# Products with v, and the transposes of their results, on two 64-row tiles with a bank each

## The chip, the core and the metric

One core of a Trainium2 chip runs the whole program in one launch. The metric is the device time of an execution in microseconds. The kernel before was timed in three runs: 2619.9, 2620.06 and 2625.03 us, median 2620.06 us. The profile is of one more execution.

## The reference

Eight sequences of 2496 rows (u and v with 256 columns, z with 64) go through an attention without softmax, and the rows that come out through a mixture of eight experts with a fixed capacity.

```python
scores = (1 / S) * np.matmul(z, z.transpose(0, 2, 1))
attn = np.maximum(scores, 0.0) ** 2
x = (u * np.matmul(attn, v)).reshape(B * S, D)
...
logits = x @ w_gate            # tokens go to experts in order of logit, at most N / E to each
out[mask] = np.maximum(x[mask] @ w1[e], 0.0) @ w2[e]
```

## The kernel before, in words

**Attention** (the first 1480 us). The work is cut into 40 groups: for each sequence b, five blocks g of queries (four of 512, one of 448). A group runs over 20 key tiles; one key tile of one group is a *step*, and there are 800 steps. I number the steps of a group 0 to 19. Every float32 product is made of two or three products of fp32r parts, a high part and what it leaves.

- `scores` (L772) makes the scores of four steps at once, four steps ahead of their use. z has 64 columns, so a key tile fills 64 rows of the array; two key tiles stand on the two halves of the rows and write to two PSUM banks. A batch is six such pairs of matmuls. Its four banks are the pool "sc".
- ScalarE turns them into `r` (relu, L790) and `a` (square, L795). `split_hi` (L798) rounds `a` to `hi`, on ScalarE for three steps of five and on VectorE for two; `split_lo` (L806) makes `lo = a - hi` on VectorE. There are three buffers of `a` and four each of `hi` and `lo`.
- `av` (L815) adds a step's products with v to two accumulators `acc0` and `acc1`, one for each half of v's 256 columns: vh·hi (L825), vh·lo (L827), vl·hi (L828), all 128 rows deep. Step 19 has no `lo` of its own and makes four matmuls, the others six. Each accumulator has two buffers, so that the next group writes to another bank.
- When a group is over, `take_acc` (L830) copies acc0 on ScalarE and acc1 on VectorE to `at0` and `at1`. Two steps later `turn_back` (L839) transposes them in eight 128x128 pieces to two sc banks, `post_mul` (L851) multiplies by u into `xs`, a DMA stores it, and `post_logits` (L868) makes 32 products `lt` of 256 columns with w_gate's rows on VectorE (L876), which are spread over the group's later steps.
- Once in a sequence `z_turn` (L730) transposes the next z in five parts, and `split_v` (L758) makes the 20 pairs `vh` (ScalarE) and `vl` (VectorE) of the next v.

The order of work is set twice: by the step for which `at(n, ...)` files each piece, and then by the framework's scheduler, which at build time gives every engine a queue of its own from that order and its own estimates. Each engine then works its queue off in order and waits where an operand or a buffer is missing.

**Experts** (from about 1480 us). For each expert VectorE searches the logits for a threshold and makes the list of its tokens: tiles `oa`, `ob` and `hl` (L415 to L425) hold one-hot codes of the rank of 40 columns of tokens each. `QW` (L201) is the number of columns that lie side by side in them: the 128 weights of one column, and the 40 numbers that move past them, are QW elements apart. 156 matmuls (L431) an expert add them up to the list. For the first expert this is on the path; for the others it runs beside the expert before, whose rows are gathered, multiplied by w1 and w2 and scattered.

Of the kernel before, what the change touches and what calls it, by code (L numbers as in the profile page):

```python
# [8 lines left out]
F32 = mybir.dt.float32  # L9
# [4 lines left out]
AF = mybir.ActivationFunctionType  # L14
# [81 lines left out]
def moe(tc, xd, first, jp, identf, w1, w2, out, B, S, cp):  # L96
    nc = tc.nc
    E, D, F = w1.shape
    NT = S // 128
    TL = S - NT * 128  # L100
    KT = NT + 1
    NG = KT // 4
    DH = D // 128
# [16 lines left out]
    with ExitStack() as ctx:  # L120
# [3 lines left out]
        ps = ctx.enter_context(tc.tile_pool(name="ps2", bufs=2, space=PSUM))  # L124
# [73 lines left out]
        nc.vector.tensor_copy(idl, idh_i)  # L198

        CB = JP // 4  # L200
        QW = 4  # L201
        QN = CB // QW
        slot = rp.tile([128, 128, QW], BF, name="slot")
        nc.gpsimd.iota(slot, pattern=[[1, 128], [0, QW]], base=0, channel_multiplier=0,  # L204
# [382 lines left out]
        todo = {}  # L587
# [4 lines left out]
        for k in range(E):  # L592
            for g in range(NG):
                n0 = (k * NG + g) * FT
# [7 lines left out]
            n0 = k * PER  # L602
# [46 lines left out]
def attention(tc, u, v, z, w_gate, xd, identf, made, first, scale):  # L649
    nc = tc.nc  # L650
    B, S, D = u.shape
    DQ = z.shape[-1]
    lg, m = first["lg"], first["m"]
    E = lg.shape[2]
    NT = S // 128
    TL = S - NT * 128
    KT = NT + 1
    DH = D // 128
# [5 lines left out]
    SCB = 4  # L664
    with ExitStack() as ctx:
# [3 lines left out]
        wk = ctx.enter_context(tc.tile_pool(name="wk", bufs=3))  # L669
        ps = ctx.enter_context(tc.tile_pool(name="ps", bufs=2, space=PSUM))  # L670
# [3 lines left out]
        def load_gate():  # L674
            wgb = wk.tile([128, E, D], F32, name="wgb", bufs=1)
            for h in range(2):
                wg = wk.tile([128, DH, 128 * E // 2], F32, name="wg", tag="xs")
                wg = wg.rearrange("p a b -> p (a b)")
                nc.sync.dma_start(wg, bass.AP(tensor=w_gate.tensor, offset=w_gate.offset + h * 128 * E,
                                              ap=[[0, 128], [1, 128 * E]]))  # L680
                with in_turn(0):
                    nc.vector.tensor_copy(wgb[:, :, h * 128:(h + 1) * 128], wg.rearrange("p (d e) -> p e d", e=E))
            wgt = wk.tile([128, DH, E], F32, name="wgt", bufs=1)
            nc.sync.dma_start(wgt, w_gate.rearrange("(h p) e -> p h e", h=DH))
            WG.update(rows=wgb, cols=wgt)
# [5 lines left out]
        ZH, ZL, ZI, ZP, VR, VH, VL, UR = {}, {}, {}, {}, {}, {}, {}, {}  # L691
        XS, ACC, AT, SC, R, A, HI, LO = {}, {}, {}, {}, {}, {}, {}, {}
# [76 lines left out]
        def width(g):  # L769
            return min(512, S - 512 * g)  # L770
# [35 lines left out]
        def split_lo(n):  # L806
            a, h = A.pop(n), HI[n]
            if seq[n][2] == NT:
                nc.vector.tensor_sub(h[TL:], a[TL:], h[TL:].bitcast(F32))
                return  # L810
            l = wk.tile([128, 512], F32R, name="lo", bufs=4)[:, :width(seq[n][1])]
            recent["l"] = nc.vector.tensor_sub(l, a, h.bitcast(F32))  # L812
            LO[n] = l

        def av(n):  # L815
            b, g, kt = seq[n]
            if kt == 0:
                ACC[b, g] = [ps.tile([128, 512], F32, name=f"acc{d}") for d in range(2)]
            last = kt == NT
            h, l = HI.pop(n), LO.pop(n, None)  # L820
            for d in range(2):
                o = ACC[b, g][d][:, :width(g)]
                c = slice(d * 128, (d + 1) * 128)
                vh, vl = VH[b, kt][:, c], VL[b, kt][:, c]
                nc.tensor.matmul(o, vh, h, start=(kt == 0), stop=False)  # L825
                if not last:
                    nc.tensor.matmul(o, vh, l, start=False, stop=False)  # L827
                nc.tensor.matmul(o, vl, h, start=False, stop=last)  # L828

        def take_acc(b, g, d):  # L830
            t = wk.tile([128, 512], F32, name=f"at{d}", bufs=2)[:, :width(g)]
            o = ACC[b, g][d][:, :width(g)]
            if d:
                nc.vector.tensor_copy(t, o)
            else:
                nc.scalar.activation(t, o, AF.Copy)
            AT[b, g, d] = t

        def turn_back(b, g):  # L839
            for half in range(2):  # L840
                p = ps.tile([128, 512], F32, name="sc", bufs=SCB)
                for i in range(2 * half, 2 * half + 2):
                    c = slice(i * 128, (i + 1) * 128)
                    if 4 * g + i == NT:
                        c = slice(i * 128 + TL - 128 * (b % 2) - TL * (1 - b % 2), i * 128 + TL)
                    for d in range(2):
                        o = p[:c.stop - c.start, (i % 2) * D + d * 128:(i % 2) * D + (d + 1) * 128]
                        nc.tensor.transpose(o, AT[b, g, d][:, c], identf)
                ACC[b, g][half] = p

        def post_mul(b, g, half):  # L851
            if half == 0:
                XS[b, g] = wk.tile([128, 4, D], F32, name="xs")
            acc = ACC[b, g][half].rearrange("p (i d) -> p i d", d=D)
            full = NT - 4 * g - 2 * half
            cuts = [(0, 2, 128)] if full >= 2 or b % 2 else [(0, full, 128), (full, 2, TL)]
            for i, j, n in cuts:
                c = slice(2 * half + i, 2 * half + j)
                nc.vector.tensor_mul(XS[b, g][:n, c], acc[:n, i:j], UR[b, g][:n, c])
            if half == 1:  # L860
                xs = XS[b, g]
                n = min(4, NT - 4 * g)
                nc.sync.dma_start(xd[b * S:b * S + NT * 128].rearrange("(p i) d -> p i d", i=NT)[:, 4 * g:4 * g + n],
                                  xs[:, :n])
                if n < 4:
                    nc.sync.dma_start(xd[b * S + NT * 128:(b + 1) * S], xs[TL * (b % 2):TL * (b % 2) + TL, n])
# [38 lines left out]
            best_expert(nc, wk, first, slice(lo, hi), eq[:, :hi - lo])  # L905
            order_keys(nc, first, slice(lo, hi))

        todo = {}

        def at(n, f, *a):  # L910
            todo.setdefault(n, []).append((f, a))
# [4 lines left out]
        for b in range(B):  # L916
            for g in range(NQ):
                n0 = (b * NQ + g) * KT
                m0 = n0 + KT
                t = m0 + (0 if m0 == B * NQ * KT else 2)  # L920
                for d in range(2):
                    at(m0, take_acc, b, g, d)
                at(t, turn_back, b, g)
                for d in range(2):
                    at(t + 1, post_mul, b, g, d)
                for e in range(4 * E if m0 < B * NQ * KT else 0):
                    at(t + 2 + e * (KT - 7) // (4 * E), post_logits, b, g, e // E, e % E)
                if b or g:
                    at(n0 - 3, load_u, b, g)
            n0 = b * NQ * KT  # L930
            if b == B - 1:
                at(B * NQ * KT + 2, last_logits, b, NQ - 1)
                at(B * NQ * KT + 3, settle, b * NT + 4 * (NQ - 1), (b + 1) * NT)
                at(B * NQ * KT + 3, settle, B * NT, J)
            if b:
                for g in range(NQ):
                    m = n0 - 3 * KT + 4 * g
                    at(m - 4, load_z, b, g)
                    at(m, z_turn, b, g)
                    at(n0 - KT + 4 * g - 8, load_v, b, g)  # L940
                at(n0 - 3 * KT + 4 * NQ + 2, swap_z, b, slice(0, KT * 128))
                for kt in range(KT):
                    at(n0 - KT + kt, split_v, b, kt)
            else:
                for kt in range(KT):
                    at(kt - 4, split_v, 0, kt)
                for g in range(1, NQ):
                    at(4 * g - LA - 1, z_turn, 0, g)
                    at(4 * g - LA, swap_z, 0, slice(512 * g, 512 * g + 512))
                    if g >= 3:  # L950
                        at(4 * g - 13, load_z, 0, g)
                        at(4 * g - 11, load_v, 0, g)
# [13 lines left out]
        start = min(min(todo), -LA)  # L966
        for n in range(-LA, N + 4 * E):
            if n == 2:
                early.close()
            if n % 4 == 0 and 0 <= n + LA < N:  # L970
                scores(n + LA)
            if 0 <= n + LA < N:
                rectify(n + LA)
            if 0 <= n + 2 < N:
                square(n + 2)
            if 0 <= n + 1 < N:
                split_lo(n + 1)
            if 0 <= n + 2 < N:
                split_hi(n + 2)
            for k in sorted(k for k in todo if k < n):  # L980
                for f, a in todo.pop(k):
                    f(*a)
            if 0 <= n < N:
                av(n)
            for f, a in todo.pop(n, []):
                f(*a)
# [25 lines left out]
```

## Time and profile before

| | us |
|---|---|
| median of three runs | 2620.06 |
| the profiled execution | 2624.11 |
| its span in the profile | 2622.1 |
| PE busy | 2540.4 |
| DVE busy | 1992.1 |
| ACT busy | 1523.7 |

The profiled execution is 4 us above the median, and inside the three runs. A matmul's time in the profile is from its start to its modelled end; matmuls overlap, so that what one costs is the distance from its start to the next one's. In the same way VectorE and ScalarE start an instruction before the one ahead has quite ended, and the cost of one is again the distance between starts. "x2" in a row of the timeline is two instructions that start together or follow each other.

### The profile page before, as it was taken

How to read it: one execution, taken by the hardware profiler on the slowest of the kernel's cores; microseconds unless marked ns; L12 is line 12 of the kernel's file. 1: busy time of each engine (PE TensorE's matmuls, PEld its weight loads, DVE VectorE, ACT ScalarE, POOL GpSimd, SP SyncE). 2: the span in 40 equal slices, each digit the busy share in tenths (PEclk: the TensorE clock that was granted, in tenths of full speed). 3: DMA queues.
4: the chain of work that ended last, by engine and by line, in shares of the span. 5: the costliest groups of instructions: out<-in, count | busy, mean ns of one | idle time of the engine just before them, and what ended most of it. 6: DMA issues, size and time to landing. Idle time of an engine off the chain costs nothing.

```text
span 2622.1 us, 44527 instructions
## 1 busy us (share of the span) xinstructions
PE 2540.4 (97%) x16035; PEld 2091.9 (80%) x16035; DVE 1992.1 (76%) x6127; ACT 1523.7 (58%) x2941; POOL 361.0 (14%) x506
## 2 busy tenths in 40 slices
PE   8999999999999999999999749999999999999998
PEld 6777777777777777777777638888989898999997
DVE  6888788887898888887888768958595969696322
ACT  7788787787787887878877412323233333233332
POOL 2000000000000000000000003233333333333331
PEclk9999999999999999999999859999999999999999
DMA  4121220220121211212100011212121212121110
GB/s 139 41 79 48 57 62 32 63 72 31 49 72 39 66 58 37 72 48 57 39 25 25 16 41 49 69 41 67 41 71 39 74 39 73 39 90 55 45 43 24
DMA packets 71645, 139.60 MB, mean 53 GB/s; under 512 B 12160, under 2 KB 39680, under 8 KB 71424
## 3 DMA queue, kind: packets, MB, share of 16 engines
q1 hardware_dynamic: 56320, 95.84, 12.2%
q0 software_dynamic: 15104, 40.91, 5.0%
q8 instruction: 126, 2.06, 0.3%
q14 instruction: 95, 0.78, 0.1%
HBM read 85.60 MB, written 40.89 MB: 48 GB/s over the span
## 4 chain that ended last, share of the span: by engine, by line
PE 82%; DVE 12%; ACT 3%; issue 2%; DMA 1%; POOL 0%; POOLq 0%; ACTq 0%; SPq 0%; DVEq 0%
PE acc L825 13%; PE acc L828 11%; PE acc L827 11%; PE sc L782 11%; PE hp L514 5%; PE y L545 5%; PE y L547 5%; PE y L546 5%; PE hp L515 5%; PE hp L516 5%; DVE lt L876 3%; DVE lo L812 2%; PE srch L431 2%; PE srch L230 2%; PE xp L499 1%
## 5 line engine op out<-in xcount | busy, mean ns | idle before, releaser
L812 DVE TENSOR_TENSOR lo<-a,hi 128x512 fp32r<-128x512 f32 (+1 forms) x760 | 508.4, 673 | 191.9 <-ACT hi L801 186.5
L825 PE MATMUL acc<-hi,vh 128*128 128x512 f32 (+1 forms) x1600 | 645.9, 404 | 1.8 <-ACT hi L801 1.8
L828 PE MATMUL acc<-hi,vl 128*128 128x512 f32 (+1 forms) x1600 | 617.9, 386 | 0.0
L827 PE MATMUL acc<-lo,vh 128*128 128x512 f32 (+1 forms) x1520 | 589.2, 388 | 0.5 <-DVE lo L812 0.2
L795 ACT ACTIVATE a<-r 128x512 f32<-128x512 f32 (+1 forms) x800 | 492.0, 631 | 145.4 <-DVE lo L812 145.4
L533 ACT ACTIVATE hh<-hp 128x512 fp32r<-128x512 f32 (+1 forms) x320 | 188.0, 588 | 562.2 <-PE hp L516 478.3
L876 DVE SCALAR_TENSOR_TENSOR lt<-xs,wgb 128x256 bf16<-128x256 f32 x1248 | 464.0, 415 | 0.5
L790 ACT ACTIVATE r<-sc 128x512 f32<-128x512 f32 (+1 forms) x800 | 426.9, 589 | 62.9 <-PE sc L782 60.5
L825 PEld LDWEIGHTS acc<-hi,vh 128*128 128x128 f32 x1600 | 300.7, 188 | 121.5 <-issue 39.5
L545 PE MATMUL y<-w2h,hh 128*128 128x256 f32 (+1 forms) x1280 | 365.1, 285 | 0.0
L546 PE MATMUL y<-w2l,hh 128*128 128x256 f32 (+1 forms) x1280 | 361.6, 283 | 0.0
L828 PEld LDWEIGHTS acc<-hi,vl 128*128 128x128 f32 x1600 | 300.9, 188 | 57.3 <-issue 0.9
L827 PEld LDWEIGHTS acc<-lo,vh 128*128 128x128 f32 x1520 | 286.3, 188 | 51.0 <-DVE lo L812 5.0
L801 ACT ACTIVATE hi<-a 128x512 fp32r<-128x512 f32 (+1 forms) x480 | 292.7, 622 | 57.8 <-PE acc L828 55.8
L514 PE MATMUL hp<-xh,w1h 128*128 128x512 f32 (+2 forms) x646 | 262.0, 406 | 0.3 <-ACT xh L507 0.3
L515 PE MATMUL hp<-xl,w1h 128*128 128x512 f32 (+2 forms) x646 | 250.4, 388 | 0.0
L516 PE MATMUL hp<-xh,w1l 128*128 128x512 f32 (+2 forms) x646 | 249.2, 386 | 0.0
L545 PEld LDWEIGHTS y<-w2h,hh 128*128 128x128 f32 (+1 forms) x1280 | 240.0, 188 | 10.3
L546 PEld LDWEIGHTS y<-w2l,hh 128*128 128x128 f32 (+1 forms) x1280 | 240.0, 187 | 9.1
L578 POOL DMA_INDIRECT out_dram<-y,idx x160 | 181.5, 1134 | 389.0 <-ACT y L572 341.5
L446 POOL DMA_INDIRECT xg<-xd,idx x160 | 160.9, 1006 | 397.9 <-PE xp L499 140.6
L204 POOL IOTA slot<- 128x512 bf16 x1 | 1.2, 1211 | 1455.1 <-DVE nrem L278 1455.1
(1144 smaller groups left out, 3793.1 us busy)
## 6 DMA issues: line engine op xcount, KB each, us to landing
vr<-in_v_dram SPq DMA_DIRECT2D x32, 512.0 KB, 3.7
ur<-in_u_dram SPq DMA_DIRECT2D x32, 512.0 KB, 4.4
xd<-xs SPq DMA_DIRECT2D x32, 512.0 KB, 2.9
wr<-in_moe_w_dram SPq DMA_DIRECT2D x32, 512.0 KB, 5.2
zh<-zh SPq DMA_DIRECT2D x14, 320.0 KB, 4.0
zl<-zl SPq DMA_DIRECT2D x14, 320.0 KB, 6.1
zin<-in_z_dram SPq DMA_DIRECT2D x31, 128.0 KB, 2.0
vr<-in_v_dram SPq DMA_DIRECT2D x8, 384.0 KB, 3.3
```

What stands on the lines that cost most here:

```text
L514: nc.tensor.matmul(p[:, c], wh, xh, start=(d == 0), stop=False)
L515: nc.tensor.matmul(p[:, c], wh, xl, start=False, stop=False)
L516: nc.tensor.matmul(p[:, c], wl, xh, start=False, stop=(d == DH - 1))
L545: nc.tensor.matmul(o, h[:, c], wh, start=first, stop=False, skip_group_check=True)
L546: nc.tensor.matmul(o, h[:, c], wl, start=False, stop=False, skip_group_check=True)
L790: recent["r"] = nc.scalar.activation(r, p, AF.Relu, scale=scale)
L795: nc.scalar.activation(a, R.pop(n), AF.Square)
L812: recent["l"] = nc.vector.tensor_sub(l, a, h.bitcast(F32))
L825: nc.tensor.matmul(o, vh, h, start=(kt == 0), stop=False)
L827: nc.tensor.matmul(o, vh, l, start=False, stop=False)
L828: nc.tensor.matmul(o, vl, h, start=False, stop=last)
L876: nc.vector.scalar_tensor_tensor(t[r], XS[b, g][r, i], 1.0, WG["rows"][r, e], op0=OP.mult, op1=OP.mult, accum_out=lg[r, j, e:e + 1])
```

## The change

The accumulators become four, each with one buffer: for either half of v's columns one bank for rows 0 to 63 of the key tile and one for rows 64 to 127. Every product with v is two matmuls on the two halves of the rows. `take_acc` becomes `take_even`, which copies the two banks of the lower half on ScalarE and is called ahead of the scores of the group's next batch, and `add_odd`, which adds the banks of the upper half to the copies on VectorE. `turn_back` transposes pieces of 64 rows, 16 a group, each half of the rows to a bank of its own, and `post_mul` reads a bank with a step. The pieces of `split_v` and the loads of v are filed over a longer stretch. `at0`, `at1`, `xs` and `wg` have fewer buffers. `QW` goes from 4 to 2.

```diff
-        QW = 4
+        QW = 2
...
-                ACC[b, g] = [ps.tile([128, 512], F32, name=f"acc{d}") for d in range(2)]
+                ACC[b, g] = [[ps.tile([128, 512], F32, name=f"acc{d}{s}", bufs=1) for s in range(2)] for d in range(2)]
...
-                vh, vl = VH[b, kt][:, c], VL[b, kt][:, c]
-                nc.tensor.matmul(o, vh, h, start=(kt == 0), stop=False)
-                if not last:
-                    nc.tensor.matmul(o, vh, l, start=False, stop=False)
-                nc.tensor.matmul(o, vl, h, start=False, stop=last)
...
+                for v, x in ((VH, h), (VH, l), (VL, h)):
+                    for s in range(2) if x is not None else ():
+                        r = slice(64 * s, 64 * s + 64)
+                        nc.tensor.matmul(ACC[b, g][d][s][:, :w], v[b, kt][r, c], x[r], start=(kt == 0 and v is VH and x is h),
+                                         stop=(last and v is VL))
+
+        def take_even(b, g):
+            for d in range(2):
+                t = wk.tile([128, 512], F32, name=f"at{d}", bufs=1)[:, :width(g)]
+                nc.scalar.activation(t, ACC[b, g][d][0][:, :width(g)], AF.Copy)
+                AT[b, g, d] = t
+
+        def add_odd(b, g):
+            for d in range(2):
+                t = AT[b, g, d]
+                nc.vector.tensor_add(t, t, ACC[b, g][d][1][:, :width(g)])
...
+                for d in range(2):
+                    for s in range(2):
+                        r = slice(64 * s, 64 * s + 64)
+                        nc.tensor.transpose(views[s][:c.stop - c.start, i, d], AT[b, g, d][r, c], identf[r, r])
...
-                XS[b, g] = wk.tile([128, 4, D], F32, name="xs")
+                XS[b, g] = wk.tile([128, 4, D], F32, name="xs", bufs=2)
...
-                    at(n0 - KT + 4 * g - 8, load_v, b, g)
+                    at(n0 - KT - 6 + 7 * g, load_v, b, g)
...
-                    at(n0 - KT + kt, split_v, b, kt)
+                    at(n0 - KT + 2 + 17 * kt // 10, split_v, b, kt)
...
+            if n in ends:
+                take_even(*ends[n])
             if n % 4 == 0 and 0 <= n + LA < N:
                 scores(n + LA)
...
+            if n in ends:
+                add_odd(*ends[n])
             if 0 <= n + 2 < N:
                 split_hi(n + 2)
```

The queues of the engines move with it. On VectorE, in the group b = 3, g = 1 of the kernel before, from the `lo` of step 6 to the `lo` of step 10 (`lt` are the products with w_gate of the group before; right ahead of these rows stand the two `xs` and three `lt`):

```order
L812 TENSOR_TENSOR lo<-a,hi 128x512
L876 SCALAR_TENSOR_TENSOR lt,lg<-xs,wgb 128x256 x2
L812 TENSOR_TENSOR lo<-a,hi 128x512
L876 SCALAR_TENSOR_TENSOR lt,lg<-xs,wgb 128x256 x6
L803 CAST hi<-a 128x512
L876 SCALAR_TENSOR_TENSOR lt,lg<-xs,wgb 128x256
L812 TENSOR_TENSOR lo<-a,hi 128x512
L803 CAST hi<-a 128x512
L876 SCALAR_TENSOR_TENSOR lt,lg<-xs,wgb 128x256
L812 TENSOR_TENSOR lo<-a,hi 128x512
L876 SCALAR_TENSOR_TENSOR lt,lg<-xs,wgb 128x256 x2
L812 TENSOR_TENSOR lo<-a,hi 128x512
```

With the change, on the same engine in the same group, from the first `lt` behind the two `xs` (the `lo` of step 6 now stands ahead of `xs`) to the `lo` of step 10:

```order
L878 SCALAR_TENSOR_TENSOR lt,lg<-xs,wgb 128x256 x6
L812 TENSOR_TENSOR lo<-a,hi 128x512
L878 SCALAR_TENSOR_TENSOR lt,lg<-xs,wgb 128x256 x13
L803 CAST hi<-a 128x512
L878 SCALAR_TENSOR_TENSOR lt,lg<-xs,wgb 128x256
L812 TENSOR_TENSOR lo<-a,hi 128x512
L878 SCALAR_TENSOR_TENSOR lt,lg<-xs,wgb 128x256 x4
L803 CAST hi<-a 128x512
L878 SCALAR_TENSOR_TENSOR lt,lg<-xs,wgb 128x256
L812 TENSOR_TENSOR lo<-a,hi 128x512
L878 SCALAR_TENSOR_TENSOR lt,lg<-xs,wgb 128x256 x6
L812 TENSOR_TENSOR lo<-a,hi 128x512
```

Of the 32 `lt` of a group, 15 stood ahead of the `lo` of step 10 and 31 stand there now. In the other groups that follow a finished one it is 31 in 24 of 39, 30 in seven, 28 in one, and 25 with six `vl` in the seven groups in which v is split.

On ScalarE, at the end of that group in the kernel before, the batch of the next group's steps 0 to 3, up to the copy of acc0 (the two `r` behind it are of the batch after):

```order
L790 ACTIVATE r<-sc 128x512 x2
L795 ACTIVATE a<-r 128x512
L790 ACTIVATE r<-sc 128x512 x2
L795 ACTIVATE a<-r 128x512
L801 ACTIVATE hi<-a 128x512
L795 ACTIVATE a<-r 128x512 x2
L801 ACTIVATE hi<-a 128x512 x2
L836 ACTIVATE at_8279<-acc_7812 128x512
L790 ACTIVATE r<-sc 128x512 x2
```

With the change, on ScalarE at the same place, with the copies of the two lower banks:

```order
L790 ACTIVATE r<-sc 128x512 x2
L795 ACTIVATE a<-r 128x512
L790 ACTIVATE r<-sc 128x512 x2
L795 ACTIVATE a<-r 128x512 x2
L801 ACTIVATE hi<-a 128x512
L795 ACTIVATE a<-r 128x512
L801 ACTIVATE hi<-a 128x512 x2
L833 ACTIVATE at_10435<-acc_9890 128x512
L833 ACTIVATE at_10437<-acc_9892 128x512
L790 ACTIVATE r<-sc 128x512 x2
```

The `hi` of step 0 has moved behind the `a` of step 2, and a second copy follows the first. On VectorE the two additions stand behind the `lo` of the next group's step 2, with one `hi` between them, where the copy of acc1 stood. On PE the six pairs of scores of the next batch stand between a group's last product and the next group's first, as before. The pieces of `split_v` stand, but for one of them, in the same group as before.

More of the change, by code (lines that the diff above doesn't have):

```diff
@@ L676, in load_gate @@
             for h in range(2):
-                wg = wk.tile([128, DH, 128 * E // 2], F32, name="wg", tag="xs")
+                wg = wk.tile([128, DH, 128 * E // 2], F32, name="wg", tag="xs", bufs=2)
                 wg = wg.rearrange("p a b -> p (a b)")
@@ L816, in av @@
             b, g, kt = seq[n]
+            w = width(g)
             if kt == 0:
-                ACC[b, g] = [ps.tile([128, 512], F32, name=f"acc{d}") for d in range(2)]
+                ACC[b, g] = [[ps.tile([128, 512], F32, name=f"acc{d}{s}", bufs=1) for s in range(2)] for d in range(2)]
             last = kt == NT
@@ L821, in av @@
             for d in range(2):
-                o = ACC[b, g][d][:, :width(g)]
                 c = slice(d * 128, (d + 1) * 128)
-                vh, vl = VH[b, kt][:, c], VL[b, kt][:, c]
-                nc.tensor.matmul(o, vh, h, start=(kt == 0), stop=False)
-                if not last:
[L827 to L837, printed above, removed]
@@ L839, in turn_back @@
-        def turn_back(b, g):
[L840 to L849, printed above, removed]
+                for v, x in ((VH, h), (VH, l), (VL, h)):
[3 more added lines that the diff above has]
+                                         stop=(last and v is VL))
@@ new lines, in take_even @@
+        def take_even(b, g):
[7 more added lines that the diff above has]
+                nc.vector.tensor_add(t, t, ACC[b, g][d][1][:, :width(g)])
+        def turn_back(b, g):
+            banks = [ps.tile([128, 512], F32, name="sc", bufs=SCB) for s in range(2)]
+            views = [p.rearrange("p (i d c) -> p i d c", d=DH, c=64) for p in banks]
+            for i in range(4):
+                c = slice(i * 128, (i + 1) * 128)
+                if 4 * g + i == NT:
+                    c = slice(i * 128 + TL - 128 * (b % 2) - TL * (1 - b % 2), i * 128 + TL)
+                for d in range(2):
+                    for s in range(2):
+                        r = slice(64 * s, 64 * s + 64)
+                        nc.tensor.transpose(views[s][:c.stop - c.start, i, d], AT[b, g, d][r, c], identf[r, r])
+            ACC[b, g] = views
@@ L851, in post_mul @@
         def post_mul(b, g, half):
             if half == 0:
-                XS[b, g] = wk.tile([128, 4, D], F32, name="xs")
-            acc = ACC[b, g][half].rearrange("p (i d) -> p i d", d=D)
-            full = NT - 4 * g - 2 * half
-            cuts = [(0, 2, 128)] if full >= 2 or b % 2 else [(0, full, 128), (full, 2, TL)]
+                XS[b, g] = wk.tile([128, 4, D], F32, name="xs", bufs=2)
+            full = NT - 4 * g
+            cuts = [(0, 4, 128)] if full >= 4 or b % 2 else [(0, full, 128), (full, 4, TL)]
@@ L857, in post_mul @@
             for i, j, n in cuts:
-                c = slice(2 * half + i, 2 * half + j)
-                nc.vector.tensor_mul(XS[b, g][:n, c], acc[:n, i:j], UR[b, g][:n, c])
+                x, y = [t[b, g][:n, i:j].rearrange("p i (d s c) -> p i d s c", s=2, c=64)[:, :, :, half] for t in (XS, UR)]
+                nc.vector.tensor_mul(x, ACC[b, g][half][:n, i:j], y)
             if half == 1:
@@ L906, in settle @@
             order_keys(nc, first, slice(lo, hi))
-        todo = {}
+        todo, ends = {}, {}
         def at(n, f, *a):
@@ L920, in attention @@
                 t = m0 + (0 if m0 == B * NQ * KT else 2)
-                for d in range(2):
-                    at(m0, take_acc, b, g, d)
+                ends[m0] = (b, g)
                 at(t, turn_back, b, g)
```

## The prediction

> **What bounds the kernel now.** I read the page first. TensorE (PE) is busy for 97% of the span and carries 82% of the chain that ended last; VectorE (DVE), at 76%, comes second.
>
> ```profile
> span 2622.1 us, 44527 instructions
> PE 2540.4 (97%) x16035; PEld 2091.9 (80%) x16035; DVE 1992.1 (76%) x6127; ACT 1523.7 (58%) x2941; POOL 361.0 (14%) x506
> PE 82%; DVE 12%; ACT 3%; issue 2%; DMA 1%; POOL 0%; POOLq 0%; ACTq 0%; SPq 0%; DVEq 0%
> ```
>
> An average hides the stages, so the next view is the busy time by window, one window in the attention and one in the experts (length, then PE, PEld, DVE, ACT, POOL, granted clock).
>
> ```profile
> 500.00:800.00 300.00, 299.80 (x1556) 230.95 (x1553) 254.52 (x855) 242.15 (x492) 0.00 (x0) 1.00 0.21 58
> 1600.00:2622.00 1022.00, 1001.34 (x7854) 910.98 (x7852) 678.24 (x1734) 326.02 (x543) 327.46 (x305) 1.00 0.17 54
> ```
>
> In both PE never stops. But in the attention VectorE is busy for 85% and ScalarE for 81% of the time. What PE gives back there counts only as far as the other two can still keep ahead of it, and that depends on the order of their queues. The third view is therefore the timeline, engine by engine, at three places: a switch of tiles, the end of a group, and the stretch behind turn_back.
>
> **The switches that go.** PE around one batch of scores:
>
> ```profile
> 606.47 0.39 PE L825 MATMUL acc<-hi,vh 128*128 128x512 f32 x1
> 606.69 0.39 PE L828 MATMUL acc<-hi,vl 128*128 128x512 f32 x1
> 607.01 0.50 PE L782 MATMUL sc<-zh 64*128 64x512 f32 x2
> 607.35 0.40 PE L782 MATMUL sc<-zl,zh 64*128 64x512 f32 x2
> ...
> 608.28 0.40 PE L782 MATMUL sc<-zh,zl 64*128 64x512 f32 x2
> 608.60 0.50 PE L825 MATMUL acc<-hi,vh 128*128 128x512 f32 x1
> 608.94 0.40 PE L827 MATMUL acc<-lo,vh 128*128 128x512 f32 x1
> ```
>
> A product of full depth follows the last after 0.23 us, and a pair of 64-row matmuls also follows a pair after 0.23 (607.35 to 608.28 is four). So a product in two halves costs PE what it cost in one piece. From full depth to pairs the two distances are 0.32 and 0.34, and the same on the way back: 0.20 us more than two times 0.23. With everything on two tiles both switches of a batch go: 200 batches x 2 x 0.20 = **-80 us**. What stays at full depth are z_turn's transposes, 39 sets of two, which now stand alone among pairs: 39 x 2 x 0.20 = 16 us at most, nothing where PE waits anyhow; I take **+10**.
>
> The halves come to 0.23 only if their weight loads run side by side. Those of the scores do (PEld, two loads in the time of one):
>
> ```profile
> 500.23 0.19 PEld L782 LDWEIGHTS sc<-zh 64*128 64x128 f32 x2
> ```
>
> **The end of a group.** acc had a second buffer; now the next group's first product writes to the banks just finished, and must wait for take_even and add_odd. Before, on ScalarE and PE:
>
> ```profile
> 637.96 1.09 ACT L790 ACTIVATE r<-sc 128x512 f32<-128x512 f32 x2 [1.72 <-PE sc L782]
> 638.93 0.63 ACT L795 ACTIVATE a<-r 128x512 f32<-128x512 f32 x1
> 639.45 1.09 ACT L790 ACTIVATE r<-sc 128x512 f32<-128x512 f32 x2
> ...
> 642.34 0.63 ACT L795 ACTIVATE a<-r 128x512 f32<-128x512 f32 x1 [0.24 <-DVE lo L812]
> 642.87 1.14 ACT L801 ACTIVATE hi<-a 128x512 fp32r<-128x512 f32 x2
> 643.91 0.58 ACT L836 ACTIVATE at<-acc 128x512 f32<-128x512 f32 x1
> ```
>
> ```profile
> 637.53 0.40 PE L782 MATMUL sc<-zh,zl 64*128 64x512 f32 x2
> ...
> 638.55 0.50 PE L825 MATMUL acc<-hi,vh 128*128 128x512 f32 x1
> ...
> 643.44 0.39 PE L828 MATMUL acc<-hi,vl 128*128 128x512 f32 x1
> ...
> 645.35 0.50 PE L825 MATMUL acc<-hi,vh 128*128 128x512 f32 x1
> ```
>
> The copy is 0.47 us behind the last product, but a chain sets its time: r, a and hi of the next group's first steps stand ahead of it. By the rows an r takes 0.48, an a 0.52, a hi 0.52, a copy 0.58. The new queue, from the same first r at 637.96, is r r a r r a a hi(0) a(3) hi hi at0 at1. hi(0) now ends at 642.10; lo(0) ends at 642.8; a(3), for which there is no fourth buffer, waits for that lo and starts at 642.85; two hi, and at0 runs from 644.41 to 644.99, at1 to 645.47. On VectorE:
>
> ```profile
> 643.52 1.30 DVE L812 TENSOR_TENSOR lo<-a,hi 128x512 fp32r<-128x512 f32 x2 [1.22 <-ACT hi L801]
> 644.73 0.68 DVE L834 COPY at<-acc 128x512 f32<-128x512 f32 x1
> 645.33 0.42 DVE L803 CAST hi<-a 128x512 fp32r<-128x512 f32 x1
> ```
>
> lo(2) needs the last hi and ends at about 645.2, so the first addition runs from 645.2 to 645.9 (0.68 as the copy, whose size it has), a hi follows, and the second ends at 646.9. PE, without switches, is done with four more pairs at 638.45, with 22 products of 0.23 at 643.45, with six pairs at 644.84, and finds the upper bank of acc0 free at 645.93. It waits 1.1 us there, and 0.3 at acc1: **1.4 us a boundary, 39 x 1.4 = +55** (1.0 if lo(2) comes sooner, 1.9 if a further lo goes ahead of it). What waits behind PE's product is the rest of its queue. In the seven groups with split_v three `vh` stand in this chain; their rows in an earlier such group are like
>
> ```profile
> 568.65 0.73 ACT L763 ACTIVATE vh<-vr 128x256 fp32r<-128x256 f32 x2
> 569.27 0.64 ACT L801 ACTIVATE hi<-a 128x512 fp32r<-128x512 f32 x1
> ```
>
> 0.31 each from start to start, which makes 0.9 us more: 7 x 0.9 = 6.5, **+7**.
>
> **Behind turn_back.** This is the largest term. Before, on VectorE and PE:
>
> ```profile
> 613.45 1.29 DVE L859 TENSOR_TENSOR xs<-sc,ur 128x512 f32<-128x512 f32 x2
> 614.66 0.41 DVE L876 SCALAR_TENSOR_TENSOR lt<-xs,wgb 128x256 bf16<-128x256 f32 x1
> 615.00 0.42 DVE L876 SCALAR_TENSOR_TENSOR lt<-xs,wgb 128x256 bf16<-128x256 f32 x1
> ...
> 622.93 0.68 DVE L812 TENSOR_TENSOR lo<-a,hi 128x512 fp32r<-128x512 f32 x1
> 623.53 0.41 DVE L876 SCALAR_TENSOR_TENSOR lt<-xs,wgb 128x256 bf16<-128x256 f32 x1
> ```
>
> ```profile
> 612.82 1.03 PE L848 MATMUL sc<-identf,at 128*128 128x128 f32 x8
> 613.61 0.48 PE L825 MATMUL acc<-hi,vh 128*128 128x512 f32 x1
> ...
> 627.13 0.39 PE L827 MATMUL acc<-lo,vh 128*128 128x512 f32 x1
> ```
>
> 622.93 is the `lo` of step 10, and 627.13 the product that reads it. VectorE's queue from xs to the end of that lo held 15 lt, five lo and two hi: 1.21 (xs) + 15 x 0.345 + 4 x 0.60 + 0.68 + 2 x 0.34 = 10.15, and the rows say 10.16. The lo lay ready 3.5 us before its use. Now the same stretch holds 31 lt, four lo and two hi: 1.21 + 10.70 + 1.80 + 0.68 + 0.68 = 15.07. PE's way to the same product was 14.31 from the transposes' start; it loses the four switches of two batches (0.8), and the first xs, which now needs all sixteen transposes (eight pairs, 0.79 as the eight before, and 0.27 to xs), begins 1.07 after that start. 14.31 - 0.80 - 1.07 = 12.44 are left. PE waits 15.07 - 12.44 = 2.6 us, 1.3 of it already for the lo of step 9 (ready at 12.33, wanted a step of 1.37 earlier, at 11.07). **39 groups x 2.6 = +101.** Bounds: 1.3 if three lt fewer stand ahead (1.0) and xs starts at once (0.3); 3.6 if xs must wait for the lo of step 6 (0.60) and each turn_back pays two switches. Behind lo(10) the queue has one lt left in most groups, and PE is caught up with, not overtaken again: lo(11) comes 0.95 later, and a step is 1.37. The last group's end has no cover, +1.
>
> **The other parts.** at, xs and wg have fewer buffers; a group lies between two uses, and nothing waits: 0. QW changes the distance of what the list matmuls read. Before, with numbers four apart (L431), and a contiguous search (L230) beside it:
>
> ```profile
> 1668.75 1.81 PE L431 MATMUL srch<-hl,ob 128*128 128x40 bf16 x40
> 1670.40 0.36 PE L545 MATMUL y<-w2h,hh 128*128 128x256 f32 x1
> ```
>
> ```profile
> 1635.47 0.42 PE L230 MATMUL srch<-mask,oh 128*128 128x48 bf16 x10
> 1635.73 0.36 PE L547 MATMUL y<-w2h,hl__20827 128*128 128x256 f32 x1
> ```
>
> One costs 1.65 / 40 = 41 ns, the other, with more columns, 26. Seven experts x 156 = 1092 such matmuls lie where PE is the bound: between 0 and -17 us; I take **-12**, nearer to the contiguous row. [...]
>
> **Sum.** -80 + 10 + 55 + 7 + 101 + 1 - 12 = +82. The profiled execution took 2624.11, 4 above the median of 2620.06; from 2624.11 I get 2706, and for the median **2702 us**.
>
> **Rivals.**
> *The late lo doesn't hold PE* (the other side). For it: VectorE has idle stretches of over 1 us in a group (the 1.22 in the row at 643.52), and a share of 85% leaves room on average. Then only the boundaries remain: 82 - 101 = -19, 2601 us; with those hidden as well, 2539. It decides where VectorE gets from xs to lo(10) within 12.4 us: 23 lt ahead instead of 31, or xs 2.6 us sooner. Against it: the queue is fixed, its idle time lies at the group's end and can't be used here. 0.10, and 0.03 for both hidden.
> *Part of it holds*, a half or less of the 101: 2602 to 2652; 0.08, half of that within 0.2%.
> [...]
> *Transposes of 64 rows in turn, not in pairs*: eight more of 0.11 a group on the way from turn_back to xs, 0.87 x 39 = +34, 2736. The row of the loads speaks against it; 0.06.
> *The switches stay*, because 64-row pairs on accumulators cost something that score pairs don't: 2782; 0.02.
>
> **How the numbers follow.** The forecast has 0.57. Its largest unknown alone (1.3 to 3.6 us a group, 51 to 140) spans 2652 to 2741; with about half of the boundaries' (39 to 74 for 55) at either end the range is 2635 to 2750, which also holds the lists and the transposes. The faster rival, the switches that stay and the lower half of the partial case, 0.19, lie outside. 0.2%, about what a measurement of this kernel can tell from no change, is 5.2 us. Faster: 0.13; within: 0.04; slower: 0.83.
>
> **What would show it.** Right: in the attention, distances from a product to a pair of scores of 0.23; PE waits of about 1.4 us at a group's first products, with add_odd (L839) named, and of 2 to 3 us at products with lo around steps 9 and 10, with L812 named; groups about 2 us longer (-2.0 for ten switches, +1.4, +2.6); L431 below 41 ns a matmul. Wrong: PE busy through the steps 8 to 11 (the walk on VectorE is wrong), lo early by the same 3.5 us, or pairs of products at more than 0.23.

## The result, and the profile after

The changed kernel takes 2819.43 us (median of four runs, 2817.55 to 2821.61) where the kernel before takes 2620.52: a ratio of 1.0758, interval 1.0742 to 1.0774, or 199 us more. The direction is the forecast one; the forecast of 2702 and its range up to 2750 are well below. The page of the profile:

```profile
span 2819.1 us, 54564 instructions
PE 2570.8 (91%) x21075; PEld 2136.3 (76%) x21075; DVE 2030.2 (72%) x6171; ACT 1548.4 (55%) x2981; POOL 368.4 (13%) x506
PE 55%; DVE 27%; ACT 13%; issue 4%; DMA 0%; POOL 0%; POOLq 0%; ACTq 0%; DVEq 0%; SPq 0%
```

PE's share of the chain fell from 82 to 55%, VectorE's rose from 12 to 27 and ScalarE's from 3 to 13. No engine is full any more: they wait for each other. The same window of the attention as before (length, then busy time of PE, PEld, DVE, ACT, POOL, granted clock) says where:

```profile
500.00:800.00 300.00, 271.07 (x2234) 212.50 (x2232) 225.35 (x738) 214.45 (x424) 0.00 (x0) 0.98 0.17 47
```

All three do less in 300 us than before. The view of the waits names what PE waited for, the four largest in the attention (us in all, times, longest); before, PE waited for `lo` for 0.2 us in the whole run:

```profile
PE acc L827 <- DVE lo L812: 75.3, 124, 1.3
PE acc L827 <- ACT at L833: 27.0, 20, 2.8
PE sc L782 <- DVE zl L750: 17.4, 16, 1.2
PE acc L827 <- DVE at L839: 14.2, 37, 0.5
```

The first product of the first group and the last of the last are 1467 us apart before (11.7 to 1479.0) and 1679 us after (11.3 to 1690.8). So the attention grew by 212 us, and what follows became 14.8 us shorter (1143.1 to 1128.3). The mean length of a group, from its first product to the next group's first, differs by its place in the sequence. I took it from the starts of L825 and L827 in each trace, for the groups from the seventh on; the last column is the start of the last product:

| us | g=0 (rest of v) | g=1 | g=2 (z parts) | g=3 | g=4 (448 wide, v) | last product |
|---|---|---|---|---|---|---|
| before | 37.1 | 36.7 | 38.4 | 36.4 | 33.7 | 1479 |
| after | 46.0 | 40.3 | 43.2 | 39.0 | 42.4 | 1691 |
| lt tied | 42.0 | 37.2 | 39.4 | 35.9 | 39.6 | 1561 |
| and v tied | 42.0 | 37.2 | 39.4 | 35.9 | 35.1 | 1529 |
| and copies first | 42.3 | 35.9 | 38.8 | 35.2 | 34.5 | 1507 |
| and settle tied | 38.0 | 37.5 | 39.3 | 35.2 | 34.5 | 1489 |
| and turn_back earlier | 37.6 | 36.9 | 38.8 | 34.6 | 34.6 | 1478 |
| and xs first | 36.0 | 36.3 | 38.8 | 34.0 | 33.3 | 1447 |
| before, with ties of lt, v and settle, and QW 2 | 36.7 | 36.7 | 37.8 | 36.4 | 34.0 | 1474 |

The rows below "after" are experiments that follow. The walk of the prediction was made for an ordinary group, and g=3, the most ordinary one, grew by 2.6 us where 2.0 were forecast (-2.0, +1.4, +2.6). g=4 and g=0 grew by 8.7 and 8.9.

**The switches are gone.** PE at the end of a group:

```profile
729.29 0.39 PE L827 MATMUL acc<-hi,vl 64*128 64x512 f32 x2
729.52 0.39 PE L782 MATMUL sc<-zh 64*128 64x512 f32 x2
729.75 0.39 PE L782 MATMUL sc<-zl,zh 64*128 64x512 f32 x2
```

From a product to the scores are 0.23 us where 0.32 and 0.34 stood, and a pair of products also takes 0.23.

**Behind turn_back**, in an ordinary group (b=3, g=3), VectorE and then PE:

```profile
781.30 0.69 DVE L812 TENSOR_TENSOR lo<-a,hi 128x512 fp32r<-128x512 f32 x1 [0.26 <-ACT hi L801]
781.91 1.28 DVE L861 TENSOR_TENSOR xs<-sc,ur 128x512 f32<-128x512 f32 x2
785.30 0.68 DVE L812 TENSOR_TENSOR lo<-a,hi 128x512 fp32r<-128x512 f32 x1
...
791.08 0.69 DVE L812 TENSOR_TENSOR lo<-a,hi 128x512 fp32r<-128x512 f32 x1
...
793.75 0.69 DVE L812 TENSOR_TENSOR lo<-a,hi 128x512 fp32r<-128x512 f32 x1
...
796.42 0.69 DVE L812 TENSOR_TENSOR lo<-a,hi 128x512 fp32r<-128x512 f32 x1
```

```profile
780.15 0.69 PE L851 MATMUL sc<-identf,at 64*128 64x64 f32 x13
...
791.82 0.50 PE L827 MATMUL acc<-lo,vh 64*128 64x512 f32 x2 [0.45 <-DVE lo L812]
794.49 0.50 PE L827 MATMUL acc<-lo,vh 64*128 64x512 f32 x2 [0.45 <-DVE lo L812]
797.16 0.50 PE L827 MATMUL acc<-lo,vh 64*128 64x512 f32 x2 [1.02 <-DVE lo L812]
```

The four rows with lo from 785.30 on are those of steps 7 to 10. From xs to the end of step 10's lo (797.11) are 15.2 us; forecast 15.07. But xs starts 1.76 us behind the transposes, not 1.07, since the lo of step 6 goes ahead of it and waits for its hi. Only the upper bound of that term counted this.

**In a group with z parts**, behind thirteen lt, VectorE, ScalarE and PE:

```profile
747.28 0.43 DVE L803 CAST hi<-a 128x512 fp32r<-128x512 f32 x1
747.62 0.41 DVE L750 TENSOR_TENSOR zl<-sc,zh 64x256 fp32r<-64x256 f32 x1
```

```profile
748.06 0.38 ACT L749 ACTIVATE zh<-sc 64x256 fp32r<-64x256 f32 x1 [4.19 <-DVE zl L750]
```

```profile
749.23 0.47 PE L782 MATMUL sc<-zh 64*128 64x512 f32 x1 [1.21 <-DVE zl L750]
```

z_turn's bank is one of the four of the scores. Its zl stands behind the run of lt, ScalarE is held for 4.19 us for the second half, and PE's batch waits for the bank. The prediction's walk followed lo alone.

**At the end of a sequence** (g=4 to g=0), ScalarE and PE:

```profile
641.68 0.63 ACT L795 ACTIVATE a<-r 128x512 f32<-128x512 f32 x1 [0.76 <-DVE lo L812]
642.22 0.40 ACT L763 ACTIVATE vh<-vr 128x256 fp32r<-128x256 f32 x1
642.52 0.61 ACT L801 ACTIVATE hi<-a 128x512 fp32r<-128x512 f32 x1
643.04 0.40 ACT L763 ACTIVATE vh<-vr 128x256 fp32r<-128x256 f32 x1
643.35 0.61 ACT L801 ACTIVATE hi<-a 128x512 fp32r<-128x512 f32 x1
643.87 0.52 ACT L833 ACTIVATE at<-acc 128x448 f32<-128x448 f32 x1
```

```profile
641.01 0.62 PE L782 MATMUL sc<-zh,zl 64*128 64x512 f32 x2
644.44 0.79 PE L827 MATMUL acc<-hi,vh 64*128 64x512 f32 x1 [2.81 <-ACT at L833]
645.38 0.79 PE L827 MATMUL acc<-hi,vh 64*128 64x512 f32 x1 [0.15 <-DVE at L839]
...
646.41 1.05 PE L827 MATMUL acc<-hi,vh 64*128 64x512 f32 x2
```

PE is ready at about 641.2 and gets both banks at 645.38: 4.1 us, where the forecast had 1.4 and 0.9 for three vh. And behind the wait a pair of products costs 0.43 us instead of 0.23. The granted clock, the last but two number of a row in the view of windows, shows why:

```profile
638.00:641.20 3.20, 3.20 (x31) 2.83 (x30) 1.75 (x5) 2.92 (x7) 0.00 (x0) 1.00 0.23 95
643.60:650.40 6.80, 5.80 (x25) 4.27 (x27) 4.66 (x10) 5.66 (x12) 0.00 (x0) 0.53 0.25 77
```

The granted clock is 0.50 from about 644.0 to 650.8. From 24 us on, this attention has fourteen such stretches, which sum up to 36 us of lost clock (one minus the granted clock, times the length); before, there is none.

### The profile page after: what moved, and what is told of

It reads as the page before. It is cut to its first block, busy times and chain, and to the rows that moved or that the text cites. A ratio compares the mean times of both kernels' runs of the same rounds, so it can differ in the third digit from the quotient of the medians.

```text
span 2819.1 us, 54564 instructions
## 1 busy us (share of the span) xinstructions
PE 2570.8 (91%) x21075; PEld 2136.3 (76%) x21075; DVE 2030.2 (72%) x6171; ACT 1548.4 (55%) x2981; POOL 368.4 (13%) x506
## 4 chain that ended last, share of the span: by engine, by line
PE 55%; DVE 27%; ACT 13%; issue 4%; DMA 0%; POOL 0%; POOLq 0%; ACTq 0%; DVEq 0%; SPq 0%
PE acc L827 18%; DVE lt L878 11%; DVE lo L812 7%; PE y L545 5%; PE hp L514 5%; ACT a L795 5%; PE y L547 5%; PE y L546 5%; PE hp L515 5%; PE hp L516 5%; ACT hi L801 4%; ACT r L790 3%; PE sc L782 3%; PE srch L230 2%; DVE hi L803 1%
## 5 line engine op out<-in xcount | busy, mean ns | idle before, releaser
L827 PE MATMUL acc<-hi,vh 64*128 64x512 f32 (+1 forms) x3200 | 806.8, 403 | 63.3 <-ACT at L833 27.0
L827 PE MATMUL acc<-lo,vh 64*128 64x512 f32 (+1 forms) x3040 | 757.2, 403 | 76.0 <-DVE lo L812 75.3
L827 PE MATMUL acc<-hi,vl 64*128 64x512 f32 (+1 forms) x3200 | 767.1, 390 | 0.0
L795 ACT ACTIVATE a<-r 128x512 f32<-128x512 f32 (+1 forms) x800 | 484.5, 629 | 321.2 <-DVE lo L812 319.5
L827 PEld LDWEIGHTS acc<-hi,vh 64*128 64x128 f32 x3200 | 426.3, 189 | 181.2 <-ACT at L833 42.7
L827 PEld LDWEIGHTS acc<-lo,vh 64*128 64x128 f32 x3040 | 401.2, 189 | 166.7 <-DVE lo L812 125.4
L827 PEld LDWEIGHTS acc<-hi,vl 64*128 64x128 f32 x3200 | 425.1, 189 | 46.9
L878 DVE SCALAR_TENSOR_TENSOR lt<-xs,wgb 128x256 bf16<-128x256 f32 x1248 | 453.1, 420 | 1.7
L545 PEld LDWEIGHTS y<-w2h,hh 128*128 128x128 f32 (+1 forms) x1280 | 240.0, 187 | 10.3
L578 POOL DMA_INDIRECT out_dram<-y,idx x160 | 188.1, 1175 | 382.5 <-ACT y L572 334.9
L782 PE MATMUL sc<-zh 64*128 64x512 f32 (+1 forms) x800 | 209.9, 396 | 27.3 <-DVE zl L750 16.6
```

What stands on the lines that cost most here:

```text
L545: nc.tensor.matmul(o, h[:, c], wh, start=first, stop=False, skip_group_check=True)
L782: nc.tensor.matmul(pair[s], key[b][r, k:k + 128], query[b][r, q], start=key is ZH and query is ZH, stop=key is ZL)
L795: nc.scalar.activation(a, R.pop(n), AF.Square)
L827: nc.tensor.matmul(ACC[b, g][d][s][:, :w], v[b, kt][r, c], x[r], start=(kt == 0 and v is VH and x is h), stop=(last and v is VL))
L878: nc.vector.scalar_tensor_tensor(t[r], XS[b, g][r, i], 1.0, WG["rows"][r, e], op0=OP.mult, op1=OP.mult, accum_out=lg[r, j, e:e + 1])
```

## The experiments

The first four were timed on a chip on which the kernel before took 2663 us and the kernels were some 43 us longer behind the attention (1171 to 1175 us in the four traces, 1128 in the trace of the changed kernel); so I compare ratios, and the starts of the last product. A tie, below, sets an instruction in its engine's order behind one that was filed just ahead of it.

**lt tied.** VectorE's order is the theory; the rivals are the 64-row work itself, and the boundaries.

```diff
+            with tc.issue_after(recent["l"].ins):
                 nc.vector.scalar_tensor_tensor(t[r], XS[b, g][r, i], 1.0, WG["rows"][r, e], op0=OP.mult, op1=OP.mult,
...
```

> The changed kernel; each lt product is only tied in VectorE's order behind the lo filed just ahead of it, so that 13 instead of 31 stand ahead of the lo of step 10. Theory (VectorE's order): in the changed kernel an ordinary group loses 3.7 us at the products of steps 7 to 10 and groups with z parts or v parts some 4 to 6 us there, about 22 us a sequence; these go: 8 x 22 = 176, about 2645 us, at most 2700. Rival 1 (64-row products are themselves dearer): no change, 2800 to 2820. Rival 2 (the single accumulators at the groups' ends and the clock drops behind them are the greater part): 2740 to 2780.

Ratio 1.0294 (1.0266 to 1.0321) instead of 1.0758: 122 us of 2620 come back, fewer than the 176 of the expectation, but the attention ends 130 us earlier and each of the five kinds of group is 2.8 to 4.0 us shorter. PE's waits, in the same view as above:

```profile
PE acc L827 <- ACT at L833: 34.0, 38, 2.6
PE acc L827 <- DVE at L839: 16.4, 39, 0.5
PE acc L827 <- DVE lo L812: 10.3, 35, 0.4
PE sc L782 <- DVE xs L861: 8.1, 11, 1.1
PE sc L782 <- DVE zl L750: 0.9, 2, 0.5
```

13 lt stand ahead of the lo of step 10 in all 39 groups, as expected. The wait for lo fell from 75.3 to 10.3 and that for zl from 17.4 to 0.9; those at the boundaries stayed. The order of VectorE is the largest cause. The 64-row work isn't: the same matmuls ran.

**v filed as before.**

```diff
-                    at(n0 - KT - 6 + 7 * g, load_v, b, g)
+                    at(n0 - KT + 4 * g - 8, load_v, b, g)
...
-                    at(n0 - KT + 2 + 17 * kt // 10, split_v, b, kt)
+                    at(n0 - KT + kt, split_v, b, kt)
```

> The changed kernel with split_v and the loads of v filed as before the change. Theory: at the end of a sequence's last group the same number of vh and vl stand in the queues either way, so nothing moves: within 15 us of 2819. Rival (the refiled pieces of v are what makes the two groups around them 8.7 us longer where others grow by 2.7): 8 x up to 12 us come back, 2720 to 2760.

Ratio 1.0764 (1.0724 to 1.0804), last product at 1688 for 1691: no difference. Refiling v did neither harm nor good: the scheduler puts the pieces together either way. In the trace with the new places and in the one with the old, the last four vh for the sequence that starts at step 400, for one, stand in the step before it.

**QW 2 alone, in the kernel before.**

```diff
-        QW = 4
+        QW = 2
```

> The kernel before with QW 2 in place of 4, nothing else. Theory (a step of 4 costs the list matmuls time): 12 to 17 us faster, about 2606. [...]

Ratio 0.9979 (0.9965 to 0.9992), 5.5 us: below the 12 to 17, on the chip with the longer experts. The groups of list matmuls of before and of this kernel (busy, mean ns):

```profile
L431 PE MATMUL srch<-hl,ob 128*128 128x40 bf16 x1092 | 48.7, 214 | 1.9 <-DVE ob L425 1.9
```

```profile
L431 PE MATMUL srch<-hl,ob 128*128 128x40 bf16 x1092 | 31.6, 181 | 4.0 <-DVE ob L425 4.0
```

17.1 us of PE's time went, so the step of 4 did cost; why less of it reached the end on that chip is not shown. The last experiment below gives 14 us.

**lt and v tied.** Beside the edit of the first experiment:

```diff
-                for i in recent.values() if b == 0 else ():
+                for i in recent.values():
```

> The first experiment, and each vh and vl tied behind the r and lo filed just ahead of it in all sequences, so that they spread over 30 steps instead of standing together. Theory (waits for vh on VectorE and three vh ahead of the copies on ScalarE make the v groups long, and the half clock follows their waits): another 8 x 8 = 64 us below the first experiment, about 2585 and under the kernel before. Rival (v's pieces are no part of it): equal to the first experiment within 10 us.

Ratio 1.0189 (1.0167 to 1.0211), 27.5 us below the first: the direction of the theory, but half its size. g=4 became 4.5 us shorter, g=0 not at all. So g=0 has another cause. In its trace ScalarE has a row with a long wait:

```profile
613.38 0.26 ACT L92 ACTIVATE rep<-key 128x72 int16<-128x72 int16 x1 [4.85 <-DVE key L81]
```

This belongs to `settle`, which ranks a finished sequence's logits: ScalarE's next r, a and hi stood behind it for 4.85 us. In the kernel before such waits for key came to 6.6 us in the whole run, in the changed one to 51.0:

```profile
ACT rep L92 <- DVE key L81: 6.6, 8, 3.9
```

```profile
ACT rep L92 <- DVE key L81: 51.0, 14, 6.1
```

In both kernels settle stands in g=0, some 25 to 28 us behind its start. Inside the attention none of its seven copies waited before; in the changed kernel all seven did, for 5.8 to 6.1 us each.

**And the copies first.** The hi of the next group's steps 1 and 2 (both are on ScalarE) go behind the copies, and the lo of step 1 behind the additions:

```diff
...
+            if n in ends and n < N:
+                with tc.issue_after(AT["last"].ins):
+                    split_hi(n + 1)
+                    split_hi(n + 2)
+                split_lo(n + 1)
...
```

> The fourth experiment, and at a group's end the hi of the next group's steps 1 and 2 tied behind the two copies of the lower banks (with the lo of step 1 behind the additions), so that the copies start when the last product is done and not two hi later. Theory (the wait at the boundary is the queue ahead of the copies): 39 x 1.0 to 1.4 = 40 to 55 us below the fourth experiment, ratio to the kernel before about 1.000. Rival (the copies only pass the wait on: hi and lo of step 1 come late instead): within 10 us of the fourth.

Ratio 1.006 (1.0043 to 1.0076), 34 us below the fourth: near the theory's 40 to 55, but by the trace only 22 of it is in the attention. The chip changed between the two, and QW 2, which both have, gave 5.5 us on the first and gives 14 in the last experiment below; that is most of the other 12. In g=3 (means of seven groups) step 0 went from 2.41 to 1.49 us, and step 3, with the batch behind it, from 3.16 to 3.96. Part of the wait moved on to there.

**And settle tied,** filed three steps earlier (at the end of g=1 instead of the start of g=2) and held there:

```diff
-            at(((b + 1) * NQ + 2) * KT, settle, b * NT, (b + 1) * NT)
+            at(((b + 1) * NQ + 2) * KT - 3, settle, b * NT, (b + 1) * NT)
...
+            with in_turn(0):
                 best_expert(nc, wk, first, slice(lo, hi), eq[:, :hi - lo])
...
```

> The fifth experiment, and the ranking of a finished sequence's logits (settle: twelve VectorE operations and a copy on ScalarE that waits for them), filed 17 steps earlier in the text but tied behind that step's lo and r, so that it comes at the end of a group instead of the middle of the run of lt. Theory: the group with it lost 4.8 us against before, 7 x 4 = 28 us below the fifth, ratio about 0.990, under both kernels. Rival (it waits the same at its new place): equal to the fifth.

Ratio 0.9998 (0.9989 to 1.0008), 16 us below the fifth: g=0 lost its 4.3 us, and g=1, where settle now is, got 1.6 back. (The expectation says 17 steps; the edit is 3. In the queue settle comes later than in the changed kernel all the same, since the scheduler had drawn it forward into g=0.) settle's copies still wait, but for 2.0 us each. The largest wait of PE that is left in the attention is now:

```profile
PE sc L782 <- DVE xs L861: 23.5, 42, 1.3
```

**The kernel before with the same ties of lt, v and settle,** and **the kernel before with one buffer for each accumulator:**

```diff
-                ACC[b, g] = [ps.tile([128, 512], F32, name=f"acc{d}") for d in range(2)]
+                ACC[b, g] = [ps.tile([128, 512], F32, name=f"acc{d}", bufs=1) for d in range(2)]
```

> The kernel before with the same ties of lt, of v's pieces and of settle, products at full depth. Theory (PE bounds it anyhow and lo lies 3.5 us ahead): no change, within 0.3%. Rival (the ties are a gain of their own, whatever the tiles): 20 us or more faster.

> The kernel before with one buffer for each accumulator instead of two. Theory (the second half's additions, not the buffer count, make the boundary wait: before, the copy on ScalarE ends at 644.49 and PE comes at 645.35, the copy on VectorE ends at 645.33 and PE comes to acc1 at 646.0): at most 0.3 us a boundary, 0 to +12 us. Rival (any group end without a second buffer costs what was forecast): +40 to +55 us.

The ties give the kernel before 0.9979 (0.9969 to 0.9989), 5 us: within what was expected, and little beside the 199 us that the ties so far took off the changed kernel (22 to 34 of them by the order at the copies, which was not tied here). One buffer for each accumulator gives 1.0007 (0.9997 to 1.0017): the count of buffers alone costs nothing that can be measured. So what costs at the boundary is taken to be the queue ahead of two copies and two additions that follow each other; the fifth experiment shows it for the queue.

**turn_back one step earlier,** and then **xs first:**

```diff
-                t = m0 + (0 if m0 == B * NQ * KT else 2)
+                t = m0 + (0 if m0 == B * NQ * KT else 1)
...
```

```diff
...
+                if "xs" in AT:
+                    turn.enter_context(tc.issue_after(AT["xs"].ins))
                 recent["l"] = nc.vector.tensor_sub(l, a, h.bitcast(F32))
```

> The sixth experiment, and turn_back and post_mul filed one step earlier. What is left of the loss in the sixth is that PE's batch behind step 3 waits for xs (its rows name it 42 times, and the step is 3.95 us where 2.75 are work): the two banks of turn_back are free only when both xs are done. Theory: the wait shrinks by up to 1.2 us a group, 39 x 0.6 to 1.2 = 25 to 47 us less, ratio 0.982 to 0.990. Rival (xs waits for the lo of step 5 ahead of it on VectorE, whenever the transposes come): equal to the sixth.

> The ninth experiment, and the lo of the steps behind step 3 tied behind the xs. Theory: the rest of the wait goes, together 39 x 1.2 = 47 us below the sixth, ratio about 0.982, PE bound again at a group of about 34 to 35 us. Rival (lo of step 4 comes late instead): not below the ninth.

The first gives 0.9945 (0.9928 to 0.9962), 14 us, fewer than the 25 to 47: PE's waits for xs fell from 23.5 to 7.0 us but not to nothing, so the rival held in part; xs still stood behind a lo. The second gives 0.9837 (0.9821 to 0.9854), together 42 us below the sixth, near the 47 expected. In that kernel xs stands ahead of the lo of step 4, and PE's batch follows without a wait:

```profile
673.49 0.68 PE L854 MATMUL sc<-identf,at 64*128 64x64 f32 x13
...
676.61 0.57 PE L830 MATMUL acc<-hi,vl 64*128 64x512 f32 x2
676.83 0.57 PE L782 MATMUL sc<-zh 64*128 64x512 f32 x2
677.06 0.57 PE L782 MATMUL sc<-zl,zh 64*128 64x512 f32 x2
```

This is the version that beats both: 2578.73 us against 2620 and 2819.

**The kernel before with the ties and QW 2,** the best of the other parts without the two tiles:

> The seventh experiment (the kernel before with the ties) with QW 2: the best that the other parts give without the two tiles. Theory: 10 to 17 us below the seventh, ratio about 0.993. Rival (the lists' matmuls are hidden by the gathers): equal to the seventh, 0.998.

2601.97 us, ratio 0.9925 (0.9908 to 0.9941), 14 us below the seventh. So with the queues in order the two tiles are worth 23 us (2578.73 against 2601.97, timed on the same chip), less than the 80 us of switches. The copies, turn_back and xs are ordered in the first of these kernels alone. In its trace PE still waits 12.0 us for the copies and 4.2 for the additions, and the groups with z parts stay 1.0 us longer than in the second (38.8 against 37.8), while g=3 is 2.4 shorter; what keeps the rest is not shown.

## Why the prediction was right or wrong

- **Switches, -80.** Right. In the kernels with ties a step with a batch takes 2.72 us and the one behind it 1.36, before 3.04 and 1.49: 0.45 a batch, 200 x 0.45 = 90.
- **z_turn between pairs, +10.** Right where nothing else waits, and near the upper bound: in g=2 a set costs 0.60 us over two steps (1.85 + 1.47 less 2 x 1.36, in the sixth experiment) and cost 0.22 before (1.61 + 1.46 less 1.49 and 1.36): 39 x 0.38 = 15. What the z parts lost beside it came from the run of lt in front of zl.
- **The ordinary boundary, +1.4 a group.** A little high: step 0 of g=3 is 2.41 for 1.36, +1.05.
- **Behind turn_back, +2.6 a group.** Right in its mechanism and its 15 us on VectorE. The steps 7 to 10 of g=3 (2.95, 2.67, 2.21 and 2.67 for 2.72 and three times 1.36) lose 3.7, just above the upper bound of 3.6, since xs started later. Step 3 of the same groups, with the batch behind the transposes, is 3.16 for 2.72, and 2.73 where xs comes first (the tenth experiment): 0.44 that the sum didn't have. With 1.05 at step 0, -2.25 for five batches and -0.28 for the transposes (0.51 for 0.79) these make the 2.6 by which g=3 grew. Over all groups the run cost not 101 but 130 us (the tie's effect on the attention, with the zl that stood behind it and 14 us of the half clock).
- **"39 groups x 2.6", "39 x 1.4" and "+7"** is the step that failed. One ordinary group was walked, and the sum taken as if the other kinds had the same queues with three vh more. g=4 and g=0 grew by 8.7 and 8.9 and g=2 by 4.8. By the ties: pieces of v between a, hi and vl that wait for each other in turn, 32 us; the order at the copies 22; settle, which the diff doesn't touch and for which ScalarE now waited, 18; and xs, behind which two of the four score banks are held, 42 (1489 to 1447, in the kernels without the other waits; in the changed kernel itself it is partly covered by them). With the 130 they make 244, and take the attention from 1691 to 1447, 32 below before. They aren't independent, so a share is that of this order of edits.
- **The half clock** had no term. 36 us of lost clock in the changed kernel, 22 with lt tied, 10 with v tied, 2 with settle tied: it goes with the waits. No run changed the clock alone, so how much of the 36 lay beside waits stays open.
- **Lists, -12.** Right: -14.8 behind the attention, and 14 in the last experiment; on the chip with the longer experts QW 2 alone gave 5.5. A list matmul went from 41 to 26 ns from start to start (40 in 1.03 us at 1871.53 of the changed kernel), and 17.1 us of PE's time went in the third experiment. That the lists gain nothing, the term at 0 and 2714 us, had 0.14; these measurements are against it.
- **The rivals.** A lo that comes late and doesn't hold PE: no, 75.3 us of named waits. Transposes in turn: no, behind the first of sixteen the next product starts 0.51 us later on one half of the rows and 0.69 on the other (780.15, 780.66 and 780.84), sooner than the 0.79 behind the eight before. Switches that stay: no.
- Why the scheduler drew the lt forward, and why settle's key now came late for ScalarE, is not shown. Its estimates for PE may count the two halves of a product one after the other, so that VectorE seems to have time; this is only argued.

## What to carry to other kernels

When the bounding engine gets faster, the order of the other engines' queues becomes the kernel: walk each kind of group, not the most ordinary one, and every instruction that the scheduler may have moved or that now comes late, also of parts that the diff doesn't name. A filler in a queue (here 32 small products) needs to be held where it was filed, or the scheduler may put all of it in front of what the bound engine wants. A bank that a helper borrows from the main loop's pool should be emptied first in its engine's queue.

## What the runs showed of the hardware that I had not expected

The granted clock fell to one half behind waits that I would have thought short: at 644.0, when PE had waited since about 641.2, until 650.8 (0.50 granted); and behind two waits of 0.95 and 0.43 us in the group that starts at 690:

```profile
691.65:695.00 3.35, 3.35 (x18) 2.50 (x16) 1.90 (x4) 2.43 (x6) 0.00 (x0) 0.51 0.02 5
```

These stretches are 3.4 and 6.8 us long; a pair of products took 0.43 in them. After waits of about 0.2 and 0.42 us (at 731) none followed. What goes with a drop can be read from the trace: its clock changes only at steps of 3.41 us. Cut at these steps, from 50 us to the last product, PE was busy (by the modelled ends) for 21 to 60% of each of the 14 pieces ahead of a drop. Of the 445 other pieces at full clock none was under 55%, and all but 12 were over 60%. From these shares I take it that the same wait counts for more or less by how it falls into these pieces; no run moved a wait within them. Two pieces ahead of a drop, and one behind which none followed:

```profile
640.54:643.95 3.41, 1.09 (x9) 0.58 (x5) 2.22 (x5) 2.65 (x7) 0.00 (x0) 1.00 0.00 0
688.33:691.74 3.41, 2.03 (x15) 0.98 (x11) 2.74 (x6) 3.41 (x8) 0.00 (x0) 1.00 0.00 0
1466.57:1469.98 3.41, 1.89 (x16) 1.18 (x16) 3.41 (x15) 2.90 (x8) 0.00 (x0) 1.00 0.00 0
```

A pair of 64-row matmuls costs what one of 128 rows does for accumulating products as well (0.23 us each). The two loads of a pair take 0.19 us together (L827 at 729.07 in the changed kernel), as the one load of 128 rows did (L825 at 606.24 before). Behind the first of sixteen 64-row transposes the next product started 0.51 us later on one half of the rows and 0.69 on the other, where eight of 128 rows had taken 0.79.
